# Decoding half of the second MoE's first matrix during the last tile of attention

## The chip, the cores and the metric

The kernel runs on one core of one Trainium2 chip. The metric is the device time of one execution in microseconds (us). A core has a matrix engine (PE, whose weight loads are listed as PEld), a vector engine (DVE), an activation engine (ACT), a general engine (POOL), and SP, which issues nearly all DMA transfers of this kernel from one queue in program order. Each engine works through its own list in order; waits between lists are semaphores.

## The reference

Attention, then two MoE blocks (plain feed-forward layers here) on the same 2304 tokens:

```python
scores = q @ k.T / 8 + bias          # q, k, v: 4 batches, 8 heads, 576 rows, 64 columns
attn   = softmax(scores)             # bias[h,i,j] = relu(x_ij * w1 + b1) @ w2, x from log distances
x = (attn @ v) reshaped to (2304, 512)
x = (silu(x @ w_gate) * (x @ w_val)) @ w_out      # 512 -> 1536 -> 512
h = relu(x @ w_in)                                 # moe2: 512 -> 2048
out = (h * h) @ w_out2                             # 2048 -> 512
```

In the trace moe2's `w_in` is `in_moe_w_in_dram`; both output matrices are called `in_moe_w_out_dram`.

## The kernel before, in words

All inputs arrive as 64-bit floats. A weight chunk of 128x512 (512 KB raw) is loaded by SP, decoded to 32-bit by three DVE instructions (`decode`, L256, L259, L261), squared for a column norm (L318 on ACT, then four small matmuls, L322), scaled by a power of two and split into two 16-bit halves (`split`, which reaches `halves` and `rest_of`: L191 on DVE, L197 and L220 on POOL, L201, L205 and L209 on ACT). The generator `first` does that for a matrix, one column block `j` of 512 at a time, four chunks `kc` each. Behind the four chunks of a block it finds one scale: a transpose (L131) and a spread (L169) on PE with a few one-column DVE instructions between them. `second` does the same for an output matrix, with one norm over the whole matrix (L355 on ACT, L139 on PE).

Attention goes over five tiles of query rows, `t` = 0, 1, 2, 3 and the merged tail `"m"` (the last 64 rows of all batches, two heads per item, 16 items). An item is: scores on PE (L804, or L799 in tile "m"), a maximum on DVE (L813), exponentials on ACT (L821), a split on ACT or POOL (L828, L825, L220), a DMA transpose of the result (L850), and the product with v (L868). `kp` and `vp` are the k and v of a pair of heads, loaded for each pair; tile "m" needs one pair per item, the tiles before one per two items. `make_bias` computes a tile's bias ahead of it with DVE masks (L595) into one of two rotating buffers of tag `bias`, each 8*576+128 words wide; the first of them also serves as a scratch room (`kvb`) in tile 0.

`finish_unit` scales and transposes 256 finished tokens into a unit `xT`; there are nine. `moe1` takes the units one by one: 288 matmuls at L453 for gate and value (twelve groups `f` of 24, each ended by ACT L461, DVE L462 and L464, and the halves on ACT L438 and POOL L220), then 72 at L476 for the output, which `out_y` writes to DRAM (L494, L495, L497). These matmuls are the filler for PE beside attention. How many of them are placed beside which part of attention is set in the program by the table `LEAD`; the order on each engine is then set by the framework, which sorts the instructions by its own timeline.

`weights2` follows the last tile. It closes attention's memory, opens `w2r` (33 chunk rooms) and `w2s` (three raw rooms), runs `first` over all four blocks of `w_in` and `second` over the 16 chunks of the output matrix, and then `combine`, which makes sums of quarters of that matrix for a fast block product. The loop at the end of the program (`hidden`, L1359 to L1368, and `outputs`, L1391) does moe2; the sums and differences of both go through the helpers at L1171, L1176 and L1178.

Of the kernel before, what the change touches and what calls it, by code (L numbers as in the profile page):

```python
# [10 lines left out]
F32 = mybir.dt.float32  # L11
F16 = mybir.dt.float16
BF16 = mybir.dt.bfloat16
I32 = mybir.dt.int32
I64 = mybir.dt.int64
# [9 lines left out]
P = 128  # L25
# [50 lines left out]
def tile_attention_moe(  # L76
# [25 lines left out]
    st = {}  # L102
# [119 lines left out]
    class Ring:  # L222


        def __init__(self, t, place):
            self.t, self.place = t, place

        def whole(self, key, j, kc):
            return self.t[:, self.place[key](j, kc) + 1, :]

        def parts(self, key, j, kc, lo, c0=0, n=512):
            o = 512 * lo + c0
            return self.t.bitcast(F16)[:, self.place[key](j, kc), o:o + n]

# [59 lines left out]
    def first(ring, mats, cols, block, sg, ahead, mm, rooms=False):  # L294


        w = sg.width
        order = [(j, key) for j in range(cols // 512) for key in mats]
        so = Source([
# [199 lines left out]

    tabT = att.tile([P, TAB + TAB2], F16, name="tabT", bufs=1)  # L500
    thetas = att.tile([P, S], F16, name="thetas", bufs=1)
# [74 lines left out]
    def make_bias(t):  # L576
# [3 lines left out]
        nh = 4 if merged else 8  # L580
        bias = att.tile([P, 8 * S + P], F32, tag="bias", name="bias")
        nc.gpsimd.memset(bias[:, 8 * S:8 * S + 1], 0.0)
# [3 lines left out]
        st["bias", t] = bias  # L586
        xs = att.tile([P, S], F32, tag="xs", name="xs", bufs=1)
        nc.sync.dma_start(xs, c_x[i0:i0 + P, :])
        masks = {}

        def mask(kb):
            m = att.tile([P, 8, P], F16, tag="mask", name="mask")
            th = theta.rearrange("p (a i) -> p a i", a=1).to_broadcast([P, 8, ni])
            for e in range(P // ni):
                nc.vector.tensor_tensor(  # L595
                    out=m[:, :, ni * e:ni * e + ni], in0=block(kb, i0, ni), in1=th, op=ALU.is_gt)
            masks[kb] = m

        def evac(kb, pv):
            cs = slice(32 * kb, 32 * kb + 32)  # L600
            tmp = att.tile([P, nh, 32], F32, tag="btmp", name="btmp")
            for e in range(8 // nh):
# [433 lines left out]
    def flat(t, o, n):  # L1036
# [11 lines left out]
        512, [wst[:, 1024 * i:1024 * i + 1024].bitcast(I64) for i in range(2)],  # L1048
        [wst[:, 2048:2304].bitcast(BF16)])
    kva = pre.tile([P, 2432], F32, name="kva")  # L1050
    kvb = att.tile([P, 8 * S + P], F32, tag="bias", name="kvb")

# [57 lines left out]
    def rest():  # L1110
# [38 lines left out]
        for i, t in enumerate((1, 2, 3, "m")):  # L1149
            gens = [(attend(2 + 2 * i, t, (0, 1, 2, 3), big, feed_of(t)), 55.0)]  # L1150
            if t != "m":
                gens.append((make_bias((2, 3, "m")[i]), 33.0))
            yield from merge(*gens)

    def w_stream():
        yield from first(
            wr, {"g": wg, "v": wv}, FF1, block_gv, sg_gv, 3, mm, True)
        kappa = []
# [52 lines left out]
    def weights2():  # L1211
        a_stack.close()
        w2p = ctx.enter_context(tc.tile_pool(name="w2p", bufs=2, side="right"))
        ps2 = ctx.enter_context(tc.tile_pool(name="ps2", bufs=5, space=PSUM))
        w2r = Ring(w2p.tile([P, 33, 512], F32, name="w2r", bufs=1), {
            "w": lambda j, kc: 4 * j + kc, "2": lambda j, kc: 16 + kc})
        st["w2p"], st["ps2"], st["w2r"] = w2p, ps2, w2r

        def mm2():
# [5 lines left out]
            [w2s[:, 3072 + 256 * i:3328 + 256 * i].bitcast(BF16) for i in range(2)])  # L1225
        yield from first(w2r, {"w": w2i}, FF2, block_rows, sg2, 3, mm2)
        kappa = []
# [10 lines left out]
        def rooms2(t, a, b=None):  # L1238
# [3 lines left out]

        st["C7"] = [rooms2(w2sh, 0), rooms2(w2sh, 3.5), rooms2(w2h, 17, 25), rooms2(new, 0), rooms2(w2h, 19, 27),
                    rooms2(wrh, 4), rooms2(wrh, 7.5), rooms2(wrh, 11)]
        st["HS"] = [wrh[:, int(1024 * o):int(1024 * o) + 3584] for o in (15, 18.5, 22, 25.5, 29, 32.5)] + [
            w2h[:, 1024 * o:1024 * o + 3584] for o in (21, 29)]
        st["yt"] = wrh[:, 0:4096]
# [223 lines left out]
```

## Time and the profile before

| | |
|---|---|
| median of three runs | 1269.7 us (1265.39, 1269.7, 1278.92) |
| span of the profiled execution, first to last instruction | 1267.5 us |
| PE busy | 1129.5 us, 89% of the span |
| DVE, ACT, POOL busy | 781.9, 681.9, 665.6 us |
| mean granted PE clock | 0.948 of full |
| DMA | 163.22 MB, mean 129 GB/s |

The page gives no time for the profiled execution other than its span; the span lies 0.2% under the median of the runs, among them. "Busy" is the time in which an engine has at least one instruction under way.

### The profile page before, as it was taken

Reading aid. Unit: us, or ns where it says so; the run is one execution under the profiler, and the core shown is the slowest. Engines: PE = TensorE matmul, PEld = TensorE weight load, DVE = VectorE, ACT = ScalarE, POOL = GpSimd, SP = SyncE. Lnnn points to the kernel's source line nnn. Section 1 sums busy time; section 2 is a strip of 40 time slices with the busy share of each in tenths; the row PEclk is TensorE's granted clock in tenths of the full one; section 3 lists DMA queues with packets and bytes.
Section 4 is the critical chain, followed back from the end, with each engine's and each line's share of the span. In section 5 each row is a group of like instructions: output and inputs, shape, how many; then the busy total and the mean of one; then the engine's idle time right before and its main releaser. Section 6 shows DMA issues by size and latency. Waiting matters only on the chain.

```text
span 1267.5 us, 27397 instructions
## 1 busy us (share of the span) xinstructions
PE 1129.5 (89%) x10550; PEld 838.5 (66%) x10550; DVE 781.9 (62%) x1872; ACT 681.9 (54%) x1386; POOL 665.6 (53%) x837
## 2 busy tenths in 40 slices
PE   2598899998869999999998896989869999999998
PEld 2476678777557678686875754766437567484787
DVE  6988747788667666566654425985685351624423
ACT  4476767547657566566664423447552542615433
POOL 1543213359858787788784530424894441705422
PEclk9688789899959999999999997999999999999999
DMA  9757643038989999998988965670010010020100
GB/s 234 201 162 182 202 113 99 14 94 178 217 200 221 221 193 189 213 191 165 185 176 196 241 154 181 180 229 27 17 34 18 18 34 34 3 48 18 26 26 18
DMA packets 278079, 163.22 MB, mean 129 GB/s; under 512 B 233276, under 2 KB 246588, under 8 KB 277948
## 3 DMA queue, kind: packets, MB, share of 16 engines
q1 hardware_dynamic: 277948, 161.46, 54.5%
q8 instruction: 83, 1.36, 0.5%
q14 instruction: 48, 0.39, 0.1%
HBM read 92.13 MB, written 19.48 MB: 88 GB/s over the span
## 4 chain that ended last, share of the span: by engine, by line
PE 46%; DMA 18%; DVE 16%; POOL 9%; issue 5%; ACT 5%; SPq 1%; POOLq 0%; ACTq 0%; DVEq 0%
PE mm L1359 11%; PE mm L1391 10%; PE mm L453 9%; DMA pT<-pt 4%; PE mm L476 4%; POOL pt L220 4%; PE qk L804 2%; DMA wr<-in_moe_w_gate_dram 2%; PE ma L1391 2%; PE av L868 2%; PE av L857 2%; DMA qT<-qs 2%; DMA kp<-kT_d 2%; DVE wr L1171 2%; DMA w2s<-in_moe_w_out_dram 1%
## 5 line engine op out<-in xcount | busy, mean ns | idle before, releaser
L453 PE MATMUL mm<-xT,wr 128*128 128x256 f16 x2376 | 293.5, 279 | 12.7 <-DVE th L464 8.5
L453 PEld LDWEIGHTS <-wr 128*128 128x128 f16 x2592 | 253.1, 100 | 60.0 <-issue 22.0
L1171 POOL TENSOR_TENSOR x<-x 128x256 f32<-128x256 f32 (+1 forms) x160 | 143.8, 909 | 175.0 <-ACT x L1368 168.8
L1359 PE MATMUL mm<-wr,w2r 128*128 128x512 f16 (+1 forms) x960 | 188.3, 358 | 8.8 <-ACT x L1364 8.8
L220 POOL TENSOR_TENSOR pt<-s,pt 128x512 f16<-128x512 f32 (+1 forms) x224 | 169.0, 776 | 31.5 <-ACT pt L828 23.7
L1359 PEld LDWEIGHTS <-w2r 128*128 128x128 f16 x960 | 93.9, 98 | 101.4 <-issue 10.0
L220 POOL TENSOR_TENSOR z<-th,z 128x256 f16<-128x256 f32 x108 | 87.5, 811 | 134.0 <-ACT z L438 124.2
L813 DVE CUSTOM_DVE_ANT_0 s<-qk,bias 128x576 f32<-128x576 f32 x144 | 108.0, 751 | 64.6 <-PE qk L804 37.0
L476 PE MATMUL mm<-wr,z 128*128 128x512 f16 x576 | 134.1, 379 | 0.0
L1391 PEld LDWEIGHTS <-wr 128*128 128x128 f16 x1134 | 111.4, 98 | 20.1 <-DVE wr L1171 3.7
L821 ACT ACTIVATE s<-s,sc 128x576 f32<-128x576 f32 x112 | 85.8, 772 | 63.7 <-DVE sc L820 52.1
L1171 DVE TENSOR_TENSOR wr<-x,wr 128x768 f16<-128x768 f32 (+3 forms) x60 | 77.9, 1309 | 65.1 <-ACT wr L1178 64.1
L476 PEld LDWEIGHTS <-z 128*128 128x128 f16 x648 | 60.0, 98 | 65.0 <-issue 0.7
L868 PE MATMUL av<-vp,pT 128*128 128x65 f16 (+5 forms) x1792 | 81.7, 196 | 19.3 <-DMA pT<-pt 18.6
L610 POOL TENSOR_TENSOR btmp<-btmp,xs 128x256 f32<-128x256 f32 (+1 forms) x90 | 67.0, 744 | 57.1 <-ACT btmp L609 54.2
L595 DVE TENSOR_TENSOR mask<-tabT,bias 128x1024 f16<-128x1024 f16 (+1 forms) x108 | 86.9, 820 | 15.8 <-PE ma L633 13.0
L868 PEld LDWEIGHTS <-pT 128*128 128x128 f16 (+3 forms) x1792 | 69.7, 101 | 36.6 <-DMA pT<-pt 24.3
L633 PEld LDWEIGHTS <-mask 128*128 128x128 f16 x1440 | 61.1, 106 | 30.6 <-DVE mask L595 12.9
L1410 ACT ACTIVATE ob<-ob,fac 128x256 f32<-128x256 f32 x36 | 17.8, 506 | 105.7 <-DVE ob L1409 105.7
L438 ACT CAST z<-th 128x256 f16<-128x256 f32 x108 | 43.0, 398 | 50.5 <-DVE th L464 48.4
L804 PE MATMUL qk<-kp,qT 128*128 128x288 f16 x384 | 65.4, 294 | 4.7 <-DMA kp<-kT_d 4.0
L1364 ACT ACTIVATE x<-mm 128x512 f32<-128x512 f32 (+1 forms) x80 | 43.1, 552 | 44.0 <-PE mm L1359 25.9
(268 smaller groups left out, 2092.9 us busy)
## 6 DMA issues: line engine op xcount, KB each, us to landing
kp<-kT_d SPq DMA_DIRECT2D x64, 288.0 KB, 3.4
vp<-v_d SPq DMA_DIRECT2D x48, 325.0 KB, 3.6
w2s<-in_moe_w_in_dram SPq DMA_DIRECT2D x16, 512.0 KB, 4.2
w2s<-in_moe_w_out_dram SPq DMA_DIRECT2D x16, 512.0 KB, 4.1
wr<-in_moe_w_gate_dram SPq DMA_DIRECT2D x24, 256.0 KB, 4.6
wst<-in_moe_w_out_dram SPq DMA_DIRECT2D x12, 512.0 KB, 4.9
wr<-in_moe_w_val_dram SPq DMA_DIRECT2D x24, 256.0 KB, 4.2
v_d<-vp SPq DMA_DIRECT2D x16, 325.0 KB, 3.2
```

Source lines behind the costliest of these rows:

```text
L220: nc.gpsimd.tensor_tensor(out=out_, in0=x, in1=hi, op=ALU.subtract)
L453: nc.tensor.matmul(pg[:, 256 * gi:256 * gi + 256], wr.parts(key, f // 4, cc, wl, P * (f % 4), P), mov(xl, cc), start=k == 0, stop=k == 11)
L476: nc.tensor.matmul(po, zall[:, f, zl, P * t:P * t + P], wr.parts("o", 0, f, wl), start=k == 0, stop=k == 3 * NF1 - 1)
L595: nc.vector.tensor_tensor(out=m[:, :, ni * e:ni * e + ni], in0=block(kb, i0, ni), in1=th, op=ALU.is_gt)
L610: nc.gpsimd.tensor_tensor(out=tmp[r], in0=tmp[r], in1=xb, op=ALU.mult)
L804: nc.tensor.matmul(pq[:, j, 0:288], qT[:, 2 * (n % 4) + s, :], kts[0][:, js], start=s == 0, stop=s == 1)
L813: nc.vector.tensor_tensor_reduce(out=s.rearrange("p (a j) -> p a j", a=2), in0=pq[:, :, 0:288], in1=bias[:, n].rearrange("p (a j) -> p a j ...
L821: nc.scalar.activation(s, s, AF.Exp, bias=nm, scale=-1.0)
L868: nc.tensor.matmul(av[r, slot, 0:cn], pT[:n, 5 * l + c, r], vs[e][c][:n, c0:c0 + cn], start=m == 0, stop=m == 13)
L1171: (nc.gpsimd if how else nc.vector).tensor_tensor(out=out_, in0=a, in1=b, op=op)
L1359: nc.tensor.matmul(ph[:, :n], w2r.parts("w", g // 4, cc, wl, P * (g % 4), P), yt[:, 4 * yl + cc, :], start=m == 0, stop=m == 11)
L1391: nc.tensor.matmul(po, HS[f][:, o:o + P], st["C7"][f][wl][:, b:b + 256], start=f == 0 and k == 0, stop=f == 7 and k == 2)
```

## The change

The two rotating bias buffers become two fixed rooms, used by the five tiles in the same turn as before; `room0` now lies in the pool `gv`, which lasts to the end. Since tile "m" uses `room1`, `room0` is free from the end of tile 3 on, and takes 8 chunks of `w_in`, blocks 0 and 1 (`w2a`). Masks, `btmp`, `xs` and the table `tabT` move into one tile `scrap`, of the same total size, which becomes the stage for these chunks: two raw rooms, where `w2s` has three. `first` for blocks 0 and 1 runs merged with the last `attend` (weights 45 and 55); `weights2` keeps blocks 2 and 3. `w2r` shrinks by 8 chunks, and places counted in it move by 8.

```diff
         def at(self, key, j, kc):
+            w = self.place[key](j, kc)
+            return w if isinstance(w, tuple) else (self.t, w)
...
-        order = [(j, key) for j in range(cols // 512) for key in mats]
+        order = [(j, key) for j in cols for key in mats]
...
-    tabT = att.tile([P, TAB + TAB2], F16, name="tabT", bufs=1)
+    BW = 8 * S + P
+    rooms = [gv.tile([P, BW], F32, name="room0"), att.tile([P, BW], F32, name="room1", bufs=1)]
+    w2a = rooms[0][:, 0:9 * 512].rearrange("p (a b) -> p a b", b=512)
+    scrap = att.tile([P, 2112 + (TAB + TAB2) // 2], F32, name="scrap", bufs=1)
+    tabT = scrap[:, 2112:2112 + (TAB + TAB2) // 2].bitcast(F16)
...
-        bias = att.tile([P, 8 * S + P], F32, tag="bias", name="bias")
+        bias = rooms[{0: 1, 1: 0, 2: 1, 3: 0, "m": 1}[t]]
...
-            m = att.tile([P, 8, P], F16, tag="mask", name="mask")
+            m = scrap[:, 512 * (kb % 2):512 * (kb % 2) + 512].bitcast(F16).rearrange("p (a i) -> p a i", a=8)
...
+    sg_e = Stage(
+        512, [scrap[:, 1024 * i:1024 * i + 1024].bitcast(I64) for i in range(2)],
+        [scrap[:, 2048 + 256 * i:2304 + 256 * i].bitcast(BF16) for i in range(2)])
...
             if t != "m":
                 gens.append((make_bias((2, 3, "m")[i]), 33.0))
+            else:
+                gens.append((first(
+                    Ring(None, {"w": lambda j, kc: (w2a, 4 * j + kc)}), {"w": w2i}, range(2), block_rows, sg_e, 2, ma), 45.0))
...
-        w2r = Ring(w2p.tile([P, 33, 512], F32, name="w2r", bufs=1), {
-            "w": lambda j, kc: 4 * j + kc, "2": lambda j, kc: 16 + kc})
+        w2r = Ring(w2p.tile([P, 25, 512], F32, name="w2r", bufs=1), {
+            "w": lambda j, kc: (w2a, 4 * j + kc) if j < 2 else 4 * j - 8 + kc, "2": lambda j, kc: 8 + kc})
...
-        yield from first(w2r, {"w": w2i}, FF2, block_rows, sg2, 3, mm2)
+        yield from first(w2r, {"w": w2i}, range(2, 4), block_rows, sg2, 3, mm2)
```

Three places of the order show what moved. The first is SP's queue at the step from tile 3 to tile "m". Before, where `kT_d_63` is the first k of tile "m":

```order
L756 DMA kp<-kT_d_66 128x1152
L748 DMA_TRANSPOSE qT<-qs 128x8x128
L759 DMA vp<-v_d_70 128x1300
L850 DMA_TRANSPOSE pT<-pt_118 128x9x128
L729 DMA qf<-in_q_dram 64x4x64
L756 DMA kp<-kT_d_63 128x1152
L729 DMA qf<-in_q_dram 64x4x64
L850 DMA_TRANSPOSE pT<-pt_119 128x9x128
L850 DMA_TRANSPOSE pT<-pt_117 128x9x128
```

And now, line numbers being those of the changed kernel (L283 loads a raw chunk, L861 is the transpose of `pt`, L767 and L770 load `kp` and `vp`):

```order
L770 DMA vp<-v_d_70 128x1300
L283 DMA scrap<-in_moe_w_in_dram 128x512
L861 DMA_TRANSPOSE pT<-pt_120 128x9x128
L767 DMA kp<-kT_d_63 128x1152
L283 DMA scrap<-in_moe_w_in_dram 128x512
L740 DMA qf<-in_q_dram 64x4x64
L861 DMA_TRANSPOSE pT<-pt_121 128x9x128
L283 DMA scrap<-in_moe_w_in_dram 128x512
L740 DMA qf<-in_q_dram 64x4x64
L861 DMA_TRANSPOSE pT<-pt_119 128x9x128
L770 DMA vp<-v_d_70 128x1300
L767 DMA kp<-kT_d_63 128x1152
```

The first load stands five transposes ahead of the first of tile "m", and the eighth ahead of the transpose of that tile's fourth item; the third to eighth wait for a decode that frees one of the two raw rooms.

The second place is SP's queue behind the last transpose of attention. Before:

```order
L850 DMA_TRANSPOSE pT<-pt_117 128x9x128
L918 DMA_TRANSPOSE xT<-xh 128x4x128 x4
L277 DMA w2s<-in_moe_w_in_dram 128x512 x5
L497 DMA y_d_77<-yh 128x1024
L277 DMA w2s<-in_moe_w_in_dram 128x512 x2
L497 DMA y_d_77<-yh 128x1024
L277 DMA w2s<-in_moe_w_in_dram 128x512 x9
L277 DMA w2s<-in_moe_w_out_dram 128x512 x9
```

And now:

```order
L503 DMA y_d_77<-yh 128x1024
L770 DMA vp<-v_d_70 128x1300
L861 DMA_TRANSPOSE pT<-pt_119 128x9x128
L503 DMA y_d_77<-yh 128x1024
L929 DMA_TRANSPOSE xT<-xh 128x4x128 x4
L283 DMA w2s<-in_moe_w_in_dram 128x512 x8
L283 DMA w2s<-in_moe_w_out_dram 128x512 x11
L503 DMA y_d_78<-yh 128x1024
```

Eight loads have gone, and both stores of `y_d_77`, the unit before the last but one, stand ahead of the loads that are left.

The third place is DVE within tile "m". Before, around the maxima (L813, shown as ISA) of two items:

```order
L462 SCALAR_TENSOR_TENSOR th<-th,mm 128x256
L464 SCALAR_TENSOR_TENSOR th<-th,mm 128x256
L813 ISA s,sc<-qk,bias 128x576
L813 ISA sc 128x1
L813 ISA s,sc<-qk,bias 128x576
L813 ISA sc 128x1
L820 TENSOR_SCALAR sc<-sc 128x1 x2
```

And now, around one item (L824 is the maximum, L262, L265 and L267 the decode of a chunk):

```order
L824 ISA s,sc<-qk,room_115 128x576
L824 ISA sc 128x1
L262 TENSOR_SCALAR room_114<-scrap 128x512
L470 SCALAR_TENSOR_TENSOR th<-th,mm 128x256
L157 TENSOR_SCALAR sc<-sc 128x1
L187 SCALAR_TENSOR_TENSOR ftok<-sc,ux 128x1
L147 TENSOR_SCALAR sc<-sc 1x1
L831 TENSOR_SCALAR sc<-sc 128x1
L265 SCALAR_TENSOR_TENSOR room_114<-scrap,room_114 128x512
L496 TENSOR_SCALAR sc<-sc 128x1
```

A decode's three instructions now stand between the small steps of attention's items.

## Rows read from the trace of the kernel before

**Rows 1.** Busy time by stage: length; PE, PEld, DVE, ACT, POOL; clock; DMA share; GB/s.

```profile
672.00:752.00 80.00, 68.24 (x954) 49.41 (x953) 32.40 (x112) 33.16 (x64) 39.05 (x56) 0.98 1.01 223
752.00:871.00 119.00, 99.96 (x770) 73.95 (x769) 91.41 (x237) 54.71 (x127) 31.32 (x31) 0.93 0.54 164
871.00:960.00 89.00, 73.12 (x382) 37.10 (x381) 61.48 (x83) 51.71 (x89) 75.08 (x66) 0.98 0.08 18
960.00:1267.50 307.50, 300.94 (x2193) 214.19 (x2190) 121.60 (x150) 127.20 (x218) 113.15 (x131) 1.00 0.09 25
```

**Rows 2.** The same view, shorter stretches.

```profile
350.00:360.00 10.00, 4.77 (x57) 3.36 (x56) 6.35 (x30) 7.62 (x18) 4.94 (x8) 0.67 0.83 174
360.00:370.00 10.00, 5.71 (x85) 5.14 (x83) 8.61 (x24) 6.56 (x15) 7.25 (x11) 0.50 0.88 202
650.00:672.00 22.00, 21.33 (x207) 13.72 (x206) 10.90 (x36) 13.69 (x31) 17.90 (x30) 1.00 0.75 152
672.00:690.00 18.00, 12.74 (x118) 7.21 (x117) 5.84 (x24) 6.91 (x13) 6.98 (x10) 0.91 1.08 236
```

**Rows 3.** The chain that ended last, between 752 and 878 us: start, length, what.

```profile
765.10 2.43 DMA xT<-xh
767.65 3.83 DMA w2s<-in_moe_w_in_dram
...
777.91 6.62 DMA y_d<-yh
...
822.88 4.53 DMA w2s<-in_moe_w_out_dram
```

**Rows 4.** PE in order of time: last product of attention, norms, scales.

```profile
750.21 1.62 PE L868 MATMUL av<-vp,pT 128*64 128x65 f16 x56
...
777.70 0.39 PE L322 MATMUL mm<-ones_b,w2s 128*128 128x1 bf16 x8
...
785.88 0.26 PE L322 MATMUL mm<-ones_b,w2s 128*128 128x1 bf16 x4 [5.00 <-ACT w2s L318]
...
821.42 0.35 PE L322 MATMUL mm<-ones_b,w2s 128*128 128x1 bf16 x8
...
871.24 0.19 PE L139 MATMUL mm<-ones_f,sc 128*1 128x1 f32 x2
```

**Rows 5.** Two lines of PE alone, L453 and then L476, in the stretch of tile "m".

```profile
672.00:752.00 80.00, 32.00 (x264) 25.41 (x264) 0.98 1.01 223
```

```profile
672.00:752.00 80.00, 12.33 (x55) 4.87 (x54) 0.98 1.01 223
```

**Rows 6.** Groups of instructions from 767 to 871 us: count, busy, mean ns, idle before.

```profile
L259 DVE SCALAR_TENSOR_TENSOR w2r<-w2s,w2r 128x512 int32<-128x512 int32 x32 | 24.5, 765 | 0.0
L261 DVE SCALAR_TENSOR_TENSOR w2r<-w2s,w2r 128x512 int32<-128x512 int32 x32 | 22.3, 700 | 0.0
L220 POOL TENSOR_TENSOR z<-th,z 128x256 f16<-128x256 f32 x20 | 19.5, 977 | 49.9 <-ACT z L438 49.8
L256 DVE TENSOR_SCALAR w2r<-w2s 128x512 int32<-128x512 int32 x32 | 16.2, 505 | 10.0 <-DMA w2s<-in_moe_w_in_dram 6.4 <-DMA w2s<-in_moe_w_out_dram 3.4
L191 DVE SCALAR_TENSOR_TENSOR w2r<-w2r,keep 128x512 f16<-128x512 f32 x10 | 7.8, 784 | 1.0 <-POOL w2r L197 1.0
L464 DVE SCALAR_TENSOR_TENSOR th<-th,mm 128x256 f32<-128x256 f32 x15 | 6.1, 410 | 0.1
L322 PE MATMUL mm<-ones_b,w2s 128*128 128x1 bf16 x64 | 3.2, 166 | 5.0 <-ACT w2s L318 5.0
```

**Rows 7.** The same view from 672 to 752 us.

```profile
L220 POOL TENSOR_TENSOR pt<-s,pt 128x512 f16<-128x512 f32 x18 | 20.8, 1156 | 14.2 <-ACT pt L828 12.7 <-PE av L868 0.9
L220 POOL TENSOR_TENSOR z<-th,z 128x256 f16<-128x256 f32 x11 | 7.7, 698 | 8.5 <-ACT z L438 8.5
```

**Rows 8.** DMA issues: KB each, median us from issue to landing.

```profile
w2s<-in_moe_w_in_dram SPq DMA_DIRECT2D x16, 512.0 KB, 4.2
```

**Rows 9.** What SP's queue waited for, 672 to 752 us: total, times, longest.

```profile
SPq L850 <- POOL pt L220: 9.9, 7, 2.4
```

More of the change, by code (lines that the diff above doesn't have):

```diff
@@ L226, in __init__, with at @@
             self.t, self.place = t, place
+        def at(self, key, j, kc):
+            w = self.place[key](j, kc)
+            return w if isinstance(w, tuple) else (self.t, w)
         def whole(self, key, j, kc):
-            return self.t[:, self.place[key](j, kc) + 1, :]
+            t, i = self.at(key, j, kc)
+            return t[:, i + 1, :]
         def parts(self, key, j, kc, lo, c0=0, n=512):
             o = 512 * lo + c0
-            return self.t.bitcast(F16)[:, self.place[key](j, kc), o:o + n]
+            t, i = self.at(key, j, kc)
+            return t.bitcast(F16)[:, i, o:o + n]
     class Stage:
@@ L586, in make_bias @@
         st["bias", t] = bias
-        xs = att.tile([P, S], F32, tag="xs", name="xs", bufs=1)
+        xs = scrap[:, 1536:1536 + S]
         nc.sync.dma_start(xs, c_x[i0:i0 + P, :])
@@ L600, in evac @@
             cs = slice(32 * kb, 32 * kb + 32)
-            tmp = att.tile([P, nh, 32], F32, tag="btmp", name="btmp")
+            o = 1024 + 256 * (kb % 2)
+            tmp = scrap[:, o:o + 32 * nh].rearrange("p (h j) -> p h j", h=nh)
             for e in range(8 // nh):
@@ L1049, in tile_attention_moe @@
         [wst[:, 2048:2304].bitcast(BF16)])
+    sg_e = Stage(
+        512, [scrap[:, 1024 * i:1024 * i + 1024].bitcast(I64) for i in range(2)],
+        [scrap[:, 2048 + 256 * i:2304 + 256 * i].bitcast(BF16) for i in range(2)])
     kva = pre.tile([P, 2432], F32, name="kva")
-    kvb = att.tile([P, 8 * S + P], F32, tag="bias", name="kvb")
+    kvb = rooms[0]
     kv_used = [0]
@@ L1156, in w_stream @@
         yield from first(
-            wr, {"g": wg, "v": wv}, FF1, block_gv, sg_gv, 3, mm, True)
+            wr, {"g": wg, "v": wv}, range(3), block_gv, sg_gv, 3, mm, True)
         kappa = []
@@ L1241, in rooms2 @@
             return t[:, a:a + 1792], t[:, b:b + 1792]
-        st["C7"] = [rooms2(w2sh, 0), rooms2(w2sh, 3.5), rooms2(w2h, 17, 25), rooms2(new, 0), rooms2(w2h, 19, 27),
+        st["C7"] = [rooms2(w2sh, 0), rooms2(w2sh, 3.5), rooms2(w2h, 9, 17), rooms2(new, 0), rooms2(w2h, 11, 19),
                     rooms2(wrh, 4), rooms2(wrh, 7.5), rooms2(wrh, 11)]
         st["HS"] = [wrh[:, int(1024 * o):int(1024 * o) + 3584] for o in (15, 18.5, 22, 25.5, 29, 32.5)] + [
-            w2h[:, 1024 * o:1024 * o + 3584] for o in (21, 29)]
+            w2h[:, 1024 * o:1024 * o + 3584] for o in (13, 21)]
         st["yt"] = wrh[:, 0:4096]
```

## The prediction

> **What bounds the kernel now.** I read the busy times by stage first [rows 1]. PE is busy 89% of the span, and from 960 us to the end it hardly rests (300.94 of 307.5), so nothing before that point can be hidden behind something else there: what is won is won as PE time that is idle earlier. From 672 us on the idle time is 11.8 us in the last tile of attention (68.24 of 80), 19.0 from there to the norm of the last matrix (99.96 of 119), and 15.9 from there to 960 (73.12 of 89). Each of the three has another limit. In tile "m" it is the memory side: DMA share 1.01 at 223 GB/s, and DVE is busy 40%. From 752 to 871 it is DVE, busy 91.41 of 119, on decodes in the main. From 871 to 960 it is POOL, 75.08 of 89. The change takes work from the second and puts it into the first.
>
> The chain of waits then shows that the decode is really on the path [rows 3]: behind attention's last product (it ends at 751.8 [rows 4]) come the transposes of unit 8, the first load of `w_in` at 767.65, decodes, a store of `y` that held ACT and PE up, and from 822.88 on the loads of the output matrix. PE in order of time gives the milestones [rows 4]: first norm of block 0 at 777.70, first norm of block 2 at 821.42, the norm of the output matrix at 871.24. Blocks 0 and 1, the ones that move, own the 43.7 us between the first two.
>
> **The change part by part.**
>
> *The stretch behind attention (752 to 871).* Removed are 8 of 32 decodes and the splits of two blocks. If everything else kept its pace, the whole 43.7 us would go: that is the most. The least is the DVE work alone: 8 chunks of 505 + 765 + 700 = 1970 ns [rows 6] are 15.8 us, 6 of the 8 splits have a DVE step of 784 ns [rows 6], 4.7 us, and some gate work moves too: between the last product of attention and the norm at L139 the new order has 453 matmuls of L453 where there were 579, five groups fewer, each with two DVE steps of 410 ns [rows 6], 4.3 us. Together 24.8 us. I take a value between them from DVE's share: 91.4 - 24.8 = 66.6 us of DVE work are left, and DVE ran at 91.41/119 = 0.77 in this stretch, which gives 86.7 us in place of 119: **-32**. PE doesn't forbid that: 453 matmuls at 32.00/264 = 0.121 us and 72 of L476 at 12.33/55 = 0.224 us [rows 5] are 71 us, and 32 norm matmuls add 1.6 (3.2/64 each [rows 6]). The 5.00 us for which PE waited at 785.88 [rows 4], behind the store of 6.62 us [rows 3], are part of what goes, since both stores of `y_d_77` now stand ahead of the loads. Bounds: -25 and -44.
>
> *The last tile (672 to 752).* Added on PE are the norms, 1.6 us, four small matmuls for the scales, 0.8 us if each is as long as L139's 0.19 [rows 4], and filler: counted from the first L799 to the last L868, the new order has 306 matmuls of L453 where there were 264 and 90 of L476 where there were 49, so 42 x 0.121 + 41 x 0.224 = 14.3 us. In sum 16.7. The idle 11.8 us are there to take it: if all of them fill, the tile grows by 5 us. Added on DMA are 8 x 512 KB = 4.2 MB, at the tile's 223 GB/s 18.8 us; if these come on top of PE's 16.7, the tile grows by 36. They don't all fall into it, though: the first loads stand five transposes ahead of the tile, where the rate was 152 GB/s at a share of 0.75 [rows 2]. From 650 to 752 some 21.2 MB were moved; 25.4 MB at the 236 GB/s of 672 to 690 [rows 2] take 107.5 us, 5.5 more than the 102. DVE gets 15.8 + 4.7 us on 32.4, still not near the tile's length; ACT and POOL, at 33.2 and 39.1, get the squares and the other steps of the splits, fewer of them. So the row nearest to it is PE's: 16.7 less a third of the idle time, **+13**; bounds +5 and +36. Each item of attention waits in turn for DVE, ACT, POOL and SP, so a part of the idle time will stay.
>
> What queues behind the new waits: on SP the transposes of `pt` and the loads of `kp` and `vp` stand behind the third to eighth load, each of which waits for a decode; on DVE the next maximum stands behind a decode that waits for its load. The loads stand two transposes apart at first, and a load lands in 4.2 us [rows 8], so I expect waits of a microsecond or two, in the 13.
>
> *From 871 to 960.* POOL's sums of quarters and differences are the same number. 105 matmuls of L453 now stand behind L139 where there were 21, 84 x 0.121 = 10.2 us more for PE, and the idle 15.9 us cover them; without that cover they would cost their 10. In the new order 18 of POOL's hidden-layer differences stand ahead of the last piece of `combine`, where there were 34, so the sums are done sooner, but all of both are needed before PE runs freely. I take **0**, with -4 and +4.
>
> *Up to 672.* The matmuls of `moe1` ahead of the first L799 are the same number as before (1728 and 414), but the order in tiles 0 and 1 is another one: the bias rooms no longer wait for a buffer to be handed over, so copies of `theta` and the first masks come earlier. There is loose time there: from 350 to 370 PE is busy 10.5 of 20 us at a clock of 0.67 and 0.50 [rows 2], which another order can lengthen or shorten. I take **0**, with -6 and +6.
>
> The sum is 13 - 32 = **-19 us**, 1248.5 against the span of 1267.5. The span lies 2.2 us under the median of the runs; I predict **1249** for a run, 1.5% less than 1269.7.
>
> **The rivals.**
>
> *More of the gain stays.* The stretch behind attention keeps its pace (-44) and the tile fills its idle time (+5): -39, **1230**. For it: 43.7 us is what the milestones show. Against: at 821.42 the decodes were nearly through with `w_in` and into the output matrix [rows 3, 4], so the pace from there on is that of a DVE that was ahead; in the new order it starts behind.
>
> *The last tile gives it all back.* DMA and PE don't overlap: +36 - 32 = +4, and half of it +20 - 32 = -12, so **1258 to 1274**, called no change. For it: share 1.01 already, and the transposes of `pt` and loads of `kp` are on the chain there. Against: PE is the busier engine, and the loads start early.
>
> *DVE and POOL get in each other's way.* Where decodes run, POOL's step for `z` takes 977 ns [rows 6], in tile "m" 698 [rows 7], and L259 takes 765 where L261 of the same shape takes 700. Some 45 POOL steps in the tile (20.8 us of them in 18 steps for `pt` [rows 7], on the path of each item) times 0.28 us are 12 us: 13 + 12 - 32 = -7, **1262**. The Trainium skill (SBUF — State Buffer, Who interferes with whom) has a rule for this that speaks against the change: a DVE instruction with two SBUF inputs and a POOL instruction that reads SBUF share a read interface, and the second to issue waits out the first. The two rows above agree with it. By that rule DVE would do its two-input decode steps better behind attention, where POOL is busy 31.32 of 119 us, than in the tile, where it is 39.05 of 80.
>
> *Slower: two raw rooms hold up SP's queue.* Six loads each wait for a decode; if SP reaches each as soon as the one before has been issued, it stands for a landing and a decode, 4.2 + 2.0 us [rows 6, 8], and attention's transposes behind it: 6 x 6.2 = 37 us, with the 13 and the -32 +18, **1287**. It is slower from the point where these waits pass 19 us, three a load. For it: SP's queue is in order, and already waits for POOL [rows 9]. Against: two or three transposes stand between loads, and an item takes 80/16 = 5 us.
>
> That the change doesn't do what it says is ruled out by the order: eight loads stand in the tile, eight behind it.
>
> **How the numbers follow.** Forecast 0.55; more gain 0.10; given back 0.14; DVE against POOL 0.10; slower 0.11. Range of the likeliest alone, from its own bounds without their extremes: 1236 to 1258. To hold 8 in 10 it is widened to the upper rival of more gain and past the middle of the two that give back: **1231 to 1267**. A measurement of this kernel can't tell less than about 1% (12.7 us) from no change. Faster by over 1%, under 1257: 0.53 of the forecast, the 0.10 above, and 0.01, so **0.64**. Within 1%: **0.24**. Slower: **0.12**.
>
> **What would show it.** In the profile after: attention's last product some 13 us later than 751.8; the norm of the output matrix (L139's counterpart) some 87 us behind it, not 119; PE idle time between the two below 15 us; POOL still the busiest engine between that norm and the last stage, about 89 us long; the first product of tile "m" within 6 us of where it was. Wrong would be: a tile "m" longer than 105 us, with SP or DVE waiting for `scrap`; or the stretch behind attention still over 105 us, with ACT or the loads of the output matrix as what ends the waits.

## The result, and the profile after

The changed kernel takes **1256.6 us** (median of 4 runs, 1252.88 to 1259.17) where the kernel before takes 1268.75 (4 runs). The ratio is **0.9895, interval 0.9857 to 0.9933**: 1.1% faster, 12 us where the forecast had 19 to 21. In seven more runs it took 1256.1 us, ratio 0.9910 (0.9878 to 0.9943). Each ratio is to runs of the kernel before that were taken beside the others, so it is not the quotient of two medians. Both intervals reach beyond 0.99: that the kernel is faster is clear, that it is faster by over 1% isn't.

The first fence is the busy times by stage of the changed kernel, with the columns of [rows 1], cut at its own milestones: first score of tile "m" (674.74), end of attention's last product (768.16), L139 (854.09), last stall of PE before the last stage (952.38), end. A few lines of code have been added, so L453, L476, L322 and L868 are L459, L482, L328 and L879 here; L139 has kept its number.

```profile
674.74:768.16 93.42, 84.00 (x1071) 58.77 (x1071) 52.83 (x173) 44.05 (x84) 48.24 (x64) 0.98 0.97 226
768.16:854.09 85.93, 73.23 (x566) 54.57 (x566) 68.77 (x173) 42.55 (x101) 20.80 (x23) 0.94 0.59 175
854.09:952.38 98.29, 85.96 (x483) 47.15 (x482) 60.98 (x91) 54.49 (x96) 77.78 (x70) 0.97 0.07 17
952.38:1256.00 303.62, 298.61 (x2171) 212.35 (x2171) 119.25 (x149) 125.87 (x216) 109.33 (x128) 1.00 0.09 25
```

The same view of the kernel before, cut at the same milestones of its own:

```profile
672.76:751.83 79.07, 67.31 (x950) 49.16 (x950) 31.51 (x109) 32.49 (x62) 39.04 (x56) 0.98 1.02 225
751.83:871.24 119.41, 100.37 (x772) 74.03 (x772) 91.76 (x237) 54.95 (x127) 31.56 (x31) 0.93 0.54 164
871.24:1267.50 396.26, 373.81 (x2570) 251.27 (x2569) 182.85 (x232) 178.67 (x306) 187.99 (x196) 0.99 0.09 23
```

The tile is 14.4 us longer, the stretch behind attention 33.5 shorter, and the rest, which I call the tail (401.91 us, the last two rows of the first fence together), 5.6 longer; with a first score 2.0 us later that is -11.5, the difference of the two spans. Now subtract the PE column from the length. PE's work from the first score on is the same, 541.5 us before and 541.8 after; what fell is its idle time, 11.8 + 19.0 + 22.5 = **53.3 us before and 9.4 + 12.7 + 17.3 = 39.5 after**. DVE's work left the second stage (91.76 to 68.77) for the first (31.51 to 52.83).

PE in order of time, as in [rows 4], the milestones of the changed kernel:

```profile
674.74 0.68 PE L810 MATMUL qk<-kp,qT 128*64 128x288 f16 x8
767.41 0.75 PE L879 MATMUL av<-vp,pT 128*64 128x65 f16 x28
788.58 0.24 PE L328 MATMUL mm<-ones_b,w2s 128*128 128x1 bf16 x4 [0.81 <-issue]
793.50 0.25 PE L328 MATMUL mm<-ones_b,w2s 128*128 128x1 bf16 x4 [0.63 <-ACT w2s L324]
854.09 0.19 PE L139 MATMUL mm<-ones_f,sc 128*1 128x1 f32 x2
860.86 5.40 PE L459 MATMUL mm<-xT,wr 128*128 128x256 f16 x48
898.26 4.41 PE L1376 MATMUL mm<-wr,w2r 128*128 128x512 f16 x12 [3.50 <-ACT x L1381]
915.04 0.83 PE L1408 MATMUL mm<-w2s,wr 128*128 128x256 f16 x6 [1.91 <-DVE wr L1188]
935.96 4.44 PE L1376 MATMUL mm<-wr,w2r 128*128 128x512 f16 x12 [3.01 <-ACT x L1381]
952.38 0.83 PE L1408 MATMUL mm<-wr,w2r 128*128 128x256 f16 x6 [0.61 <-ACT w2r L1195]
```

The first norm behind attention is now that of block 2 (788.58), and the wait of 5.00 us in [rows 4] is gone. The last of the 105 mixed products behind L139 are those at 860.86, and they end at 866; PE's first idle time behind L139 comes at 894.8, 29 us later. That is where the forecast's tail went wrong (below).

The chain that ended last, behind attention, as in [rows 3] (start, length, what): no store of `y` stands in it any more, and the first load of the output matrix listed stands at 803.53, 35.4 us behind the last product, where it stood 71.1 behind (822.88 against 751.8). SP issues these loads from 800.52 on, 32.4 us behind the last product, and from 813.31 on before, 61.5 behind.

```profile
778.81 2.49 DMA xT<-xh
781.95 4.00 DMA w2s<-in_moe_w_in_dram
790.38 3.74 DMA w2s<-in_moe_w_in_dram
797.91 4.54 DMA w2s<-in_moe_w_in_dram
803.53 4.17 DMA w2s<-in_moe_w_out_dram
```

### The profile page after: what moved, and what is told of

The parts are those of the page before. It is cut to its first block, busy times and chain, and to the rows that moved or that the text cites. A ratio compares the mean times of both kernels' runs of the same rounds, so it can differ in the third digit from the quotient of the medians.

```text
span 1256.0 us, 27398 instructions
## 1 busy us (share of the span) xinstructions
PE 1129.9 (90%) x10550; PEld 833.4 (66%) x10550; DVE 779.8 (62%) x1872; ACT 682.8 (54%) x1386; POOL 653.2 (52%) x837
## 4 chain that ended last, share of the span: by engine, by line
PE 51%; DMA 13%; DVE 9%; POOL 5%; issue 4%; ACT 3%; SPq 1%; POOLq 0%; ACTq 0%; DVEq 0%
PE mm L459 13%; PE mm L1376 12%; PE mm L1408 10%; PE mm L482 4%; DMA pT<-pt 4%; PE av L879 3%; PE qk L815 2%; DMA qT<-qs 2%; POOL x L1188 2%; PE ma L1408 2%; DMA scrap<-in_moe_w_in_dram 2%; DMA w2s<-in_moe_w_out_dram 1%; PE ma L644 1%; POOL pt L220 1%; DMA w2s<-in_moe_w_in_dram 1%
## 5 line engine op out<-in xcount | busy, mean ns | idle before, releaser
L459 PE MATMUL mm<-xT,wr 128*128 128x256 f16 x2400 | 292.3, 278 | 11.6 <-DVE th L470 4.6
L459 PEld LDWEIGHTS <-wr 128*128 128x128 f16 x2592 | 253.4, 100 | 55.9 <-issue 15.7
L220 POOL TENSOR_TENSOR pt<-s,pt 128x512 f16<-128x512 f32 x224 | 173.0, 795 | 39.5 <-ACT pt L839 33.7
L482 PE MATMUL mm<-wr,z 128*128 128x512 f16 x612 | 142.5, 379 | 0.8 <-DVE th L470 0.8
L824 DVE CUSTOM_DVE_ANT_0 s<-qk,room 128x576 f32<-128x576 f32 x144 | 107.7, 749 | 43.1 <-PE qk L815 27.1
L1376 PE MATMUL mm<-wr,w2r 128*128 128x512 f16 (+1 forms) x480 | 103.2, 366 | 6.5 <-ACT x L1381 6.5
L482 PEld LDWEIGHTS <-z 128*128 128x128 f16 x648 | 59.8, 98 | 66.1 <-issue 1.9
L605 DVE TENSOR_TENSOR scrap<-scrap,room 128x1024 f16<-128x1024 f16 (+1 forms) x108 | 85.6, 807 | 27.5 <-PE ma L644 23.0
L1376 PE MATMUL mm<-wr,room 128*128 128x512 f16 (+1 forms) x480 | 100.1, 358 | 0.0
L879 PE MATMUL av<-vp,pT 128*128 128x65 f16 (+5 forms) x1792 | 82.3, 196 | 19.7 <-DMA pT<-pt 18.3
L879 PEld LDWEIGHTS <-pT 128*128 128x128 f16 (+3 forms) x1792 | 69.3, 101 | 39.0 <-DMA pT<-pt 24.4
L621 POOL TENSOR_TENSOR scrap<-scrap 128x256 f32<-128x256 f32 (+1 forms) x90 | 63.5, 706 | 53.6 <-ACT scrap L620 50.0
L1376 PEld LDWEIGHTS <-w2r 128*128 128x128 f16 x480 | 47.7, 99 | 54.3 <-issue 10.5
L1376 PEld LDWEIGHTS <-room 128*128 128x128 f16 x480 | 47.1, 98 | 45.8 <-issue 0.5
L644 PEld LDWEIGHTS <-scrap 128*128 128x128 f16 x1440 | 60.6, 105 | 24.4 <-DVE scrap L605 10.6
```

The lines of the kernel that those rows point to most:

```text
L220: nc.gpsimd.tensor_tensor(out=out_, in0=x, in1=hi, op=ALU.subtract)
L459: nc.tensor.matmul(pg[:, 256 * gi:256 * gi + 256], wr.parts(key, f // 4, cc, wl, P * (f % 4), P), mov(xl, cc), start=k == 0, stop=k == 11)
L482: nc.tensor.matmul(po, zall[:, f, zl, P * t:P * t + P], wr.parts("o", 0, f, wl), start=k == 0, stop=k == 3 * NF1 - 1)
L605: nc.vector.tensor_tensor(out=m[:, :, ni * e:ni * e + ni], in0=block(kb, i0, ni), in1=th, op=ALU.is_gt)
L621: nc.gpsimd.tensor_tensor(out=tmp[r], in0=tmp[r], in1=xb, op=ALU.mult)
L644: nc.tensor.matmul(pv[:, :, :, c:c + 4], m[:, a, :], bd[:, l], start=l == 0, stop=l == 1)
```

## The experiments

All runs in one table. Stages are from one profile each, cut as above; "idle" is PE's idle time from the first score of tile "m" to the end, "behind" the number of mixed products (L453) that the program puts behind L139.

| kernel | median us | ratio to before (interval) | tile | to L139 | tail | idle | behind |
|---|---|---|---|---|---|---|---|
| before | 1268.75 | | 79.1 | 119.4 | 396.3 | 53.3 | 21 |
| changed | 1256.62 | 0.9895 (0.9857 to 0.9933) | 93.4 | 85.9 | 401.9 | 39.5 | 105 |
| changed, again | 1256.10 | 0.9910 (0.9878 to 0.9943) | 93.8 | 86.5 | 401.9 | 39.4 | 105 |
| nothing early | 1267.18 | 0.9993 (0.9963 to 1.0023) | 82.8 | 121.8 | 393.2 | 52.6 | 10 |
| one block early | 1258.05 | 0.9900 (0.9866 to 0.9934) | 81.8 | 101.0 | 401.0 | 43.7 | 54 |
| before, stores on ACT's queue | 1269.50 | 0.9989 (0.9959 to 1.0019) | 78.9 | 119.9 | 395.5 | 50.6 | 21 |
| six early loads out | 1255.41 | 0.9872 (0.9834 to 0.9909) | 91.6 | 85.4 | 401.7 | 37.4 | 105 |
| weight 25 | 1264.61 | 0.9971 (0.9944 to 0.9999) | 89.0 | 93.0 | 409.4 | 48.0 | 183 |
| 8 sums on DVE | 1251.07 | 0.9878 (0.9839 to 0.9917) | 94.8 | 86.0 | 398.8 | 40.6 | 105 |
| 16 sums on DVE | 1250.07 | 0.9852 (0.9815 to 0.9890) | 94.9 | 86.3 | 397.7 | 37.4 | 105 |
| one block, 8 sums on DVE | 1259.88 | 0.9938 (0.9913 to 0.9963) | 83.8 | 102.1 | 403.5 | 45.6 | 54 |
| lead table lowered | 1261.72 | 0.9946 (0.9917 to 0.9975) | 89.4 | 93.3 | 395.3 | 42.9 | 31 |
| the same, 16 sums on DVE | 1260.89 | 0.9973 (0.9945 to 1.0000) | 94.6 | 93.9 | 394.0 | 47.6 | 31 |
| before, 16 sums on DVE | 1262.90 | 0.9973 (0.9940 to 1.0006) | 77.4 | 119.0 | 394.7 | 47.2 | 21 |

The idle column nearly sorts the medians: 37 to 41 us go with 1250 to 1257, 43 to 48 with 1258 to 1265, over 50 with 1267 and more.

**Nothing early.** All four blocks behind attention, in the rooms and the order of the change.

```diff
-            else:
-                gens.append((first(Ring(None, {"w": ...}), {"w": w2i}, range(2), block_rows, sg_e, 2, ma), 45.0))
...
-        yield from first(w2r, {"w": w2i}, range(2, 4), block_rows, sg2, 3, mm2)
+        yield from first(w2r, {"w": w2i}, range(4), block_rows, sg2, 3, mm2)
```

> The changed kernel with its rooms, scraps and order of tiles kept, but all four row blocks of the second MoE's first matrix are loaded, decoded and split behind attention, as before. Theory 1 (the gain is the decode of eight chunks leaving the stretch behind attention and running beside the last tile): the gain goes; 1264 to 1272 us, the last attention product back near 752 us and the last weight norm's product about 115 to 121 us behind it. Theory 2 (the gain comes from the rooms and the changed order of tiles, not from when the matrix is decoded): the gain stays, 1254 to 1260 us.

1267.2 us: no difference from the kernel before. Its stages lie within 3.7 us of those of before; the tile is the one furthest off, at a granted clock of 0.90 in this profile and 0.98 before. Theory 2 falls; the rooms, the scrap tile and the new order of tiles 0 and 1 are worth nothing by themselves, and the whole gain is the early decode.

**One block early.**

```diff
-                    ... {"w": w2i}, range(2), block_rows, sg_e, 2, ma), 45.0))
+                    ... {"w": w2i}, range(1), block_rows, sg_e, 2, ma), 45.0))
...
-        yield from first(w2r, {"w": w2i}, range(2, 4), block_rows, sg2, 3, mm2)
+        yield from first(w2r, {"w": w2i}, range(1, 4), block_rows, sg2, 3, mm2)
```

> The changed kernel with only the first of the four row blocks early, and the other three behind attention. Theory 1: about half of what two blocks do at each place: last attention product 7 to 9 us later than in the kernel before, the stretch from it to the last weight norm's product about 102 us (119 before, 86 changed), 54 products of the mixed values behind that instead of 105, so that the tail loses 2 to 3 us instead of 5.6; 1260 to 1265 us. Theory 2: as the changed kernel, 1254 to 1260 us. If the queue of loads behind attention, rather than the decode, set the stretch, one block would win under 3 us.

The stretch behind attention came out as expected (101.0), the whole did not: 1258.05 us, within 2 us of two blocks. Here is its stage view, with the same three cuts as the kernel before above.

```profile
671.68:753.44 81.76, 73.77 (x1013) 52.93 (x1013) 41.49 (x142) 39.03 (x74) 43.07 (x61) 1.00 1.02 229
753.44:854.48 101.04, 85.72 (x676) 63.47 (x677) 79.89 (x208) 48.71 (x115) 26.16 (x27) 0.97 0.57 172
854.48:1255.50 401.02, 380.62 (x2603) 255.06 (x2602) 179.79 (x235) 179.75 (x308) 188.65 (x197) 0.98 0.09 23
```

The first block takes 18.4 us off the stretch and lengthens the tile by 2.7, since PE's 6.5 us of filler find 3.8 us of idle time there. The second takes off another 15.1 and lengthens the tile by 11.7: its 10.2 us of PE work find none, and the tile's idle time even rises from 8.0 to 9.4. With 0.9 in the tail the second block wins 2.6 us from the first score on, 1.4 to 2.0 by the medians, which these runs can't tell from nothing. "About half at each place" takes it that PE's room in the tile is shared evenly; what of it gets filled, the first block fills.

**The two stores on another queue.** In the kernel before.

```diff
-        nc.sync.dma_start(y_d[m][P * t:P * t + P, :], ...)
+        (nc.scalar if m == 6 else nc.sync).dma_start(y_d[m][P * t:P * t + P, :], ...)
```

> The kernel before, with nothing moved but the issue of two stores: the two of the store tile that stood behind the loads of the matrix on SyncE's queue go out on ScalarE's queue. Theory 3 (the gain is these stores, whose wait stood in the chain of the kernel before, getting free of the loads): 1260 to 1263 us, 6 to 8 us faster than before. Theory 1: the decode chain takes over at once; 1264 to 1270 us, at most 4 us faster.

No gain, but it doesn't price the wait either, since the wait is still there. First the chain behind attention in this kernel, then two rows of PE in order of time:

```profile
766.56 3.78 DMA w2s<-in_moe_w_in_dram
...
776.79 6.63 DMA y_d<-yh
```

```profile
779.42 0.24 PE L322 MATMUL mm<-ones_b,w2s 128*128 128x1 bf16 x4
784.70 0.27 PE L322 MATMUL mm<-ones_b,w2s 128*128 128x1 bf16 x4 [5.04 <-ACT w2s L318]
```

The store goes out from ACT's queue at once and still releases its waiter 6.63 us later, as it did after 6.62 from SP's queue [rows 3], while the sixteen stores of this kernel on SP's queue have a median of 2.7 us. So its place in SP's queue is not what held it up; loads of `w_in` are in flight beside it in both kernels. They can't be all of it, though: the second of the two stores goes out beside such loads too, and it landed after 3.2 us from ACT's queue and 2.5 from SP's. The Trainium skill (DMA: Bandwidth & Descriptors, Issuing engines are not separate DMA queues) says that transfers started by different engines run on the same 16 DMA engines and interleave; the two rows agree. What the wait of 5.0 us was worth stays open: it is part of the 33.5, and no run takes it away alone.

**Six early loads left out.**

```diff
-                    nc.sync.dma_start(r[n * i:n * i + n], a)
+                    if sg is not sg_e or self.loaded < 2:
+                        nc.sync.dma_start(r[n * i:n * i + n], a)
```

> The changed kernel with six of the eight early chunk loads left out (the decode runs on what the first two brought, so the output is not the reference's). If the last tile of attention grows by the products that the planner puts into it (theory 1), it stays at 92 to 94 us from its first score to its last attention product, and the whole at 1254 to 1259 us. If it grows by the loads, which share the DMA engines with the loads of the last tile, the tile falls to 79 to 86 us and the whole to 1245 to 1251 us.

The tile still takes 91.6 us with a DMA share of 0.90 instead of 0.97, and the whole 1255.4, within a microsecond or so of the changed kernel. Against the two profiles of the changed kernel (93.4 and 93.8) the tile is 1.9 to 2.3 us shorter, so these six loads make little of its 14.4 us. The decodes, the splits and PE's filler all stay in this run, and it doesn't tell these apart.

```profile
673.08:764.65 91.57, 83.38 (x1060) 59.07 (x1060) 50.88 (x168) 44.53 (x84) 46.38 (x62) 0.94 0.90 197
```

**Weight 25 for the early decode.**

```diff
-                    ... range(2), block_rows, sg_e, 2, ma), 45.0))
+                    ... range(2), block_rows, sg_e, 2, ma), 25.0))
```

> The changed kernel with the weight of the early matrix in the planner's merge at 25 instead of 45: the early decode has to be done within fewer of the last tile's steps of the planner, so the planner puts 64 and not 90 products of the first MoE's output and 288 and not 306 of its mixed values into the tile, and 183 mixed products instead of 105 stand behind the last weight norm's product. Theory A (what is left of the gain is the idle time of PE; the work moved only shifts where PE is busy, and PE's idle time behind the last weight norm stays at 17 to 20 us however many products stand ahead of it): tile 5 to 8 us shorter, stretch behind attention about the same, tail 6 to 10 us longer; 1255 to 1262 us. Theory B (the tail has room for moved products): the tail grows by under 3 us and the whole falls to 1248 to 1252 us.

The expectation has the weight the wrong way round: in `merge` a smaller weight gives a generator fewer turns. With 25 the second block's norms come at 769 to 772 us, behind attention's last product, and its rest stands ahead of blocks 2 and 3; so the stretch grows by 7.1 us as well, the tile falls by 4.4 and not 5 to 8, and the whole gives most of the gain back, 1264.6 where theory A had 1262 at most. The tail went as theory A says: 78 more products behind L139 make it 7.5 us longer, and PE's idle time there stays at 17.4. Theory B falls: the 78 products found no free room in the tail.

**Sums moved from POOL to DVE.** `hidden` has four sums a block, all on POOL; of the first eight blocks one or two are put on DVE.

```diff
-    ... "s": (1,), ...
+    ... "s": (1, 0, 1, 1) * 8 + (1,) * 128, ...      # 8 sums; (1, 0, 1, 0) for 16
```

> The changed kernel with one of the four sums of each of the first eight hidden blocks of the second MoE on VectorE instead of GpSimd (eight sums of 1.07 us off GpSimd, between about 900 and 950 us). Theory A (behind the last weight norm a chain of elementwise work, GpSimd's foremost, sets the pace up to about 952 us, so that the 84 products moved there could not fill its idle time): the tail of 401.9 us falls by 3 to 8 us, PE's 17.3 us idle there by as much; 1249 to 1254 us. Theory B (PE's own work sets that stretch): within 1.5 us of the changed kernel, 1255 to 1258 us. If VectorE becomes the one that is late: 1257 to 1262 us.

> The changed kernel with two of the four sums of each of the first eight hidden blocks on VectorE (16 sums, 17 us off GpSimd). Theory A with GpSimd as the pace: 1 to 3 us faster again than with one sum, 1247 to 1253 us. If VectorE, ScalarE and the waits between the engines take over as the pace after the first eight sums: no better than with one, or up to 4 us slower.

> One row block early, as in the experiment before, and the eight sums on VectorE. Theory A: its tail of 401.0 us, with 20.4 us of idle time on PE, falls by 4 to 9 us; 1249 to 1254 us, no more than 2 us from the two blocks with the same sums moved. Theory B: 1257 to 1260 us, as with one block alone.

With two blocks early the tail shrinks by 3.1 us with 8 sums and by 4.2 with 16 (PE's idle time in it by 2.1 and 3.1), and the whole to 1251.1 and 1250.1: inside both expectations, though the sizes show that POOL is only part of the pace. Groups of instructions from 850 to 943 us with 16 sums (the stretch before the last stage), on POOL and on DVE, line, operation, count, busy, mean ns, idle before:

```profile
L1188 POOL TENSOR_TENSOR x<-x 128x256 f32<-128x256 f32 x16 | 16.5, 1044 | 10.4 <-ACT x L1385 6.7 <-DVE x L1188 3.4
```

```profile
L1188 DVE TENSOR_TENSOR x<-x 128x256 f32<-128x256 f32 x16 | 13.8, 882 | 4.7 <-ACT x L1385 4.1 <-POOL x L1188 0.6
```

POOL lost 17 us of work there and the tail 4, and POOL now waits for ACT and for the sums on DVE. That fits a chain through three engines, not one engine that sets the pace; no run isolates it. With one block early the same eight sums won nothing (1259.9, tail 2.5 us longer): theory B's time, where theory A wanted 4 to 9 us off the tail.

The two long waits of PE for ACT's `x` (3.5 us at 898.26, 3.0 at 935.96) can be followed back on ACT. First the Relu that the kernel before runs first behind L139, then the two Relus of the changed kernel that end these waits:

```profile
904.05 2.06 ACT L1364 ACTIVATE x<-mm 128x512 f32<-128x512 f32 x4 [2.01 <-DMA y_d<-yh]
```

```profile
897.61 2.06 ACT L1381 ACTIVATE x<-mm 128x512 f32<-128x512 f32 x4 [2.92 <-DMA y_d<-yh]
935.31 1.09 ACT L1381 ACTIVATE x<-mm 128x512 f32<-128x512 f32 x2 [3.07 <-DVE wr L1188]
```

The first waits for the last store of `y`, in both kernels: `hidden` gets its `x` from the pool `wk`, which is opened where the memory of `moe1` has just been closed. The second waits for DVE's differences of an earlier block. With 8 sums on DVE PE's waits for ACT's `x` are as long as without (6.6 and 6.5 us in all), with 16 they are 4.2.

**The lead table lowered.** This asks for the forecast's tail directly: it brings 74 of the 84 products back in front of L139, and 24 mixed and 18 output products (6.9 us at 0.121 and 0.224 [rows 5]) further forward still, ahead of tile "m".

```diff
-LEAD = [0, 39, 78, 117, 260, 400], [0, 85.669, 132.183, 165.544, 287.094, 406.094]
+LEAD = [0, 39, 78, 117, 260, 400], [0, 85.669, 132.183, 165.544, 282.094, 401.094]
```

> The changed kernel with the last two points of the planner's lead table lowered by 5, which brings 74 of the 84 products that had moved behind the last weight norm back in front of it: 31 mixed products stand there instead of 105 (21 in the kernel before). Theory A (those products cost the tail because they stand ahead of a chain of elementwise work in which PE sits idle, and the whole is PE's work plus PE's idle time): the tail falls from 401.9 to 393 to 397 us, what lies ahead grows by about as much, PE's idle time from the first score of the last tile to the end stays at 37 to 42 us, and the whole at 1253 to 1260 us. Theory B (the forecast's tail of 396.3 us was to be had, and only their place cost 5.6 us): 1249 to 1252 us.

> Both at once: the lead table of the kernel beside it, and two of the four sums of the first eight hidden blocks on VectorE. Theory A: as the sums alone (1250.1 us, PE idle 37.4 us), 1247 to 1253 us. Theory B: 3 to 6 us below that, 1244 to 1247 us.

> The kernel before with the 16 sums on VectorE and nothing else. If the idle time behind the last weight norm is there in both kernels for the same reason (GpSimd's sums, 33.9 us of them in the 91.5 us up to 962.7 us), this wins as much as on the changed kernel: 3 to 7 us, 1261 to 1266 us where the kernel before has 1268. If it is a debt of the early blocks alone, under 1.5 us.

```profile
678.75:768.13 89.38, 80.57 (x1078) 60.72 (x1078) 60.06 (x180) 44.83 (x87) 48.80 (x62) 0.98 1.01 240
768.13:861.40 93.27, 75.92 (x591) 57.04 (x591) 69.83 (x170) 41.83 (x100) 19.70 (x25) 0.95 0.55 158
861.40:1256.70 395.30, 378.57 (x2580) 254.15 (x2579) 182.12 (x231) 178.87 (x305) 187.42 (x194) 0.98 0.09 24
```

That view shows the swap: against the changed kernel the tail falls by 6.6 us to 395.3, below the forecast's, and the stretch behind attention grows by 7.3, of which 2.7 us are PE's work and 4.7 its idle time; the first score comes 4.0 later and the tile is 4.0 shorter. PE's idle time is 42.9 us, 3.4 more than in the changed kernel, and the median 1261.7 is 5 us worse and just past theory A's end. Theory B falls: the shorter tail is to be had, but not for nothing. With the 16 sums on top (1260.9) neither theory's time came; the tail fell by 1.3 more. In the kernel before, the 16 sums give 1262.9, an interval that reaches 1.0006, and a tail 1.5 us shorter in the profile: what the sums are worth without the early blocks can't be told from nothing here.

**The changed kernel again.**

> The changed kernel itself once more, in as many rounds as the kernels that are held against it, since its own median (1256.6 us) stands on four runs. If the second early block and the 16 sums are worth what the medians say, it lies between one block (1258.05 us) and the 16 sums (1250.07 us), at 1255 to 1259 us, with its last weight norm about 86 us behind the last attention product and a tail of 400 to 403 us. A median of 1253 us or less would leave the 16 sums without a gain of their own; one of 1260 us or more would make one block the better version.

As expected: 1256.1 us, stages within 0.6 us of the first profile, a tail of 401.9 in both; only the first score comes 3.8 us earlier. Of all kernels the 16 sums on the changed kernel are the fastest, 1250.07 us, 1.5% under the kernel before. Its interval and the changed kernel's (0.9815 to 0.9890; 0.9857 to 0.9933 and 0.9878 to 0.9943) overlap a little, so 6 us over the change are likely, not proved. Of these 6, the profiles show 2.3 to 3.2 behind the first score (579.0 us from there to the end, 581.3 and 582.2 without the sums); the first score, which lies ahead of all these sums, comes at 669.50, and at 674.74 and 670.95 without them.

## Why the prediction was right, and where its size was off

*What bounds the kernel.* "What is won is won as PE time that is idle earlier" is what the runs show: PE's work from the first score on is 541.5 and 541.8 us, and the idle time fell by 13.8. That this idle time falls because of the early decode is shown by taking only that away (nothing early: 52.6 us idle, no gain).

*The stretch behind attention:* -32 forecast, -33.5 measured. The method, DVE's remaining work at its own share of the stretch, was close: 66.6 us forecast and 68.77 measured, at a share of 0.77 forecast and 68.77/85.93 = 0.80 measured. But DVE alone doesn't set this stretch. In the chain that ended last, loads are 33% between 768 and 860 us and the three decode steps 25.5% (21% and 26.4% before, between 752 and 878), and with the lead table lowered 69.83 us of DVE work took 93.27, a share of 0.75. That the share held so well here is in part luck.

*The last tile:* +13 forecast, +14.4 measured. PE's work grew by 16.7 us, as forecast, and 2.3 of them, not 3.9, found idle time; the third of the idle time that was to be filled was taken, not derived. "In tile "m" it is the memory side" doesn't hold for what was added: the run without six loads shows that it isn't their DMA time. That PE's filler is the rest of it is argued from PE's 84.0 busy us of 93.4; the decode steps between attention's items were in every run that had the filler.

*The tail, the step that failed.* "84 x 0.121 = 10.2 us more for PE, and the idle 15.9 us cover them" was priced at 0, with +4 as its bound, and measured +5.6: PE's busy time grew by 10.8 (373.81 to 384.57), and its idle time fell by only 5.1 (22.5 to 17.3). The cover was the right length and in the wrong place. The moved products end at 866 us, and PE first idles at 894.8, when it waits for the Relu that waits for the last store of `y`. Up to that idle time PE is busy without a gap in both kernels, so the moved products put this Relu off by their whole length: it comes 32.8 us behind L139 before and 43.5 in the change, 10.7 later. From the Relu to the end, before and after, with the columns of [rows 1]:

```profile
904.05:1267.50 363.45, 342.32 (x2412) 235.97 (x2411) 165.17 (x186) 159.46 (x267) 166.75 (x176) 0.99 0.09 24
```

```profile
897.61:1256.00 358.39, 343.90 (x2412) 236.01 (x2411) 154.84 (x179) 156.25 (x263) 155.65 (x168) 0.99 0.09 24
```

This part is 5.1 us shorter, with as many matmuls: DVE and POOL have 10.3 and 11.1 us less left to do in it, since they worked on beside the moved products. So 10.7 - 5.1 makes the 5.6. The other kernels agree on the whole: with the Relu 31.0, 32.1, 32.8, 40.5, 43.5 and 55.1 us behind L139 (lead table lowered, nothing early, before, one block, changed, weight 25) 364.3, 361.2, 363.5, 360.5, 358.4 and 354.3 us follow it, so a later start is paid back by some 0.4 of the delay. No run moves the store or the room of `x` by itself, so this is read from the traces and not tested. Lowering the lead table shows that the products can be moved back, and that the tail's 6.6 us then come back as 7.3 in the stretch behind attention; why 4.7 of these are idle time stays open.

*Up to 672:* 0 forecast, +2.0 measured in this profile, first score at 670.95 in the second one, 672.76 before: the bound of 6 held, and the change's part in it is less than what two profiles of one kernel differ by.

*The rivals.* More of the gain stays: the stretch stops at -33.5, and PE takes its filler from it. The last tile gives it all back: for the first block it gives back 2.7 of 18.4 us, but for the second 11.7 of 15.1, so in size this rival came near for half of the change. Its mechanism, DMA time on top of PE's, is what the run without six loads speaks against. DVE and POOL in each other's way: the rows below, groups on POOL in the changed kernel's tile, answer to [rows 7].

```profile
L220 POOL TENSOR_TENSOR pt<-s,pt 128x512 f16<-128x512 f32 x18 | 21.6, 1201 | 13.4 <-ACT pt L839 12.7
L220 POOL TENSOR_TENSOR z<-th,z 128x256 f16<-128x256 f32 x12 | 10.2, 847 | 22.3 <-ACT z L444 16.8 <-PE av L879 5.4
```

The steps for `pt` take 1201 ns (1156 before), those for `z` 847 (698), together 18 x 0.045 + 12 x 0.149 = 2.6 us and not the rival's 12; POOL's two other groups in the tile add 1.1 (the 128x64 steps 353 ns, 315 before; L836 712, 671 before). The Trainium skill's rule (SBUF — State Buffer, Who interferes with whom) has the direction of these rows, not a size that mattered. L259 beside L261, which the prediction counted with it, says nothing on it, since both steps read two SBUF inputs. Raw rooms holding up SP's queue: of SP's waits from 660 to 768 us (total, times, longest) these are all that the loads have, 0.7 us in three and not six of 6.2; the last row is the longest with a decode as its end, and it belongs to a transpose of `xT`.

```profile
SPq L283 <- DVE sc L166: 0.3, 1, 0.3
SPq L283 <- DVE sc L150: 0.2, 1, 0.2
SPq L283 <- DVE room L267: 0.2, 1, 0.2
SPq L929 <- DVE room L262: 3.8, 1, 3.8
```

The waiting was the other way round, DVE's for the loads, over the same time:

```profile
DVE room L262 <- DMA scrap<-in_moe_w_in_dram: 8.7, 5, 3.7
```

Of "what would show it" all came but one: last product 16.3 us later than 751.8 (13 forecast), L139 85.9 behind it (87), idle time between them 12.7 (under 15), first product 2.0 us off (within 6). POOL is busiest of the three side engines up to 952 (77.78 of 98.29), but that stretch is 98 us long, not 89, with the 105 products at its head.

## What to carry to other kernels

Where one engine's total work doesn't change, count its idle time before and after, stage by stage; that difference is the gain, and a stage that got shorter by sending work elsewhere is not. Idle time covers added work only if the work can stand between the waits: look at when in the stage the gaps come, not only at their sum, and at what waits for the added work to end (here the last store of `y`, and through it the first block of the next matrix). Move such a thing in the smallest piece first, since the first piece may use up the free room (here one block of two brought 10 or 11 of the 12 us).

## What the hardware showed that I had not expected

A 256 KB store released its waiter 6.63 us after its issue on ACT's queue and 6.62 us after that on SP's, beside loads of `w_in`, where the stores on SP's queue take 2.7 us in the median: another queue did not shield it. The next store, beside such loads as well, landed 3.2 and 2.5 us after its issue, so what held the first one up stays open. And a sum of 128x256 32-bit numbers (`x`) cost 0.88 us on DVE and 1.04 on POOL while both worked on such sums; the sums for `t`, of the same shape and in the same stretch of that run, cost 0.60 and 0.62 on DVE and 0.98 and 0.83 on POOL, so 0.88 against 1.04 is a figure of that mix and not of the two engines.
